# Attention from q and k laid out by the host with the head dimension first, scores as 64-row fp32 products

## The chip, the cores and the metric

One core of one Trainium2 chip runs the program. The metric is the device time of one execution in microseconds (us). The kernel before took 1429.79 us, the median of three runs (1424.49 to 1429.9). The profiled execution used below took 1432.03 us; its span from the first to the last instruction is 1429.9 us.

## The reference

Retention-like attention over 8 sequences of 576 tokens with 8 heads of 64, then two expert layers (8 experts each, 512 to 1024 to 512) on the 4608 tokens. The first layer routes each token to its best expert; the second deals tokens to experts by sorted logits with a fixed capacity. Only the first part is touched:

```python
scores = scale * np.matmul(q, k.transpose(0, 1, 3, 2))
gamma = 1.0 - 2.0 ** (-5.0 - np.arange(H, dtype=np.float32))
rel = pos[:, None] - pos[None, :]
Dmat = np.where(rel >= 0, gamma[:, None, None] ** rel[None, :, :], 0.0)
x = np.matmul(scores * Dmat[None], v)          # [B, H, S, D]
x = x.transpose(0, 2, 1, 3).reshape(B * S, H * D)
x = moe2(moe(x))
```

## The kernel before

The 4608 tokens are 36 tiles of 128; nine tiles make two sequences, so tile 4 of each nine holds the end of one sequence and the start of the next. Inside a tile the scores are computed in full; what came earlier in the sequence enters through a 64 x 64 state per head that the tiles accumulate in PSUM (`st`) and that ScalarE copies into the block-diagonal `bd`.

The order on every engine is the order in which the program is written. A tile passes through these steps, and the loop over T (L526) mixes the steps of different tiles:

- `load_tile` (L225) queues on SyncE three loads of k, q, v (rows = tokens, pieces of 64 words). It runs three tiles ahead; each of the three has four buffers.
- `s_tr` (L292): GpSimd makes `kd` (k times a decay, L298). TensorE transposes k and q by head pairs (L304, eight transposes into two PSUM tiles `tp`). ScalarE and VectorE split the transposed k and q into a high and a low fp32r part (L307, L308, L312, L315); q's two heads are put on zeroed halves, `QP`, which borrows the weight tiles w2_0 and w2_1.
- `s_qk` (L327): for each of the four head pairs three fp32r products (high-high, high-low, low-high) of 128 rows by 256 columns into `s0`, `s1` (L338), twelve in all. VectorE multiplies by the decay table `dt` into `sm` (L342).
- `s_qs` (L319): VectorE makes `qs`, the decayed transposed q (L325).
- `s_pv` (L345): state times query (L353, four fp32 products) and v times `sm` (L357, eight fp32 products, the two heads of a pair on two column halves). ScalarE copies the result to `xT` (L360).
- `s_state` (L363): eight fp32 products add the tile to the state (L375), ScalarE copies it to `bd` (L381).
- `s_out` (L384): four router products of 32 columns (L395) into the PSUM bank `lg`, four transposes of `xT` (L401), ScalarE copies and the sum of squares. `s_sel` (L407): one small product (L410) sums the router's parts into logits.
- `route`, pulled step by step by `pump` (L486), turns a group of five tiles into slots; GpSimd scatters the rows to `xs` (L471). After the fifth group SyncE loads the early rows of expert 0 (`load_x`, L480).

At T = 31 the first four weight loads of the experts are queued (`w_load`, L552), and at T = 31 to 34 ScalarE and GpSimd convert one each (`w_conv`, L180 and L181). After the loop come the last routing steps, an overflow test that reads a value into all engines, and the expert layers from about 257 us on.

The eight PSUM banks of the stage hold: `lg` one, `tp` three, `s0`, `s1`, `o`, `st` one each.

## Time and profile before

| | us | 
|---|---|
| median of three runs | 1429.79 |
| profiled execution, device time | 1432.03 |
| its span | 1429.9 |
| attention, main stretch | 40 to 220 |
| attention and routing, last part | 206 to 257 |
| expert layers | 257 to 1430 |

Engines are PE (TensorE products), PEld (its weight loads), DVE (VectorE), ACT (ScalarE), POOL (GpSimd) and SP (SyncE, which issues loads). A busy share says how long an engine had an instruction in work. Durations of products include the way through the array and overlap; the distance between the starts of one group and the next tells what a group costs. An fp32 product leaves two records, a transpose and an fp32r product one. PEclk is the clock granted to TensorE; 1.00 is 2.4 GHz and 0.50 is 1.2 GHz.

### The profile page before, as it was taken

What the parts mean: (1) busy time and instruction counts of PE and PEld (TensorE: products, weight loads), DVE (VectorE), ACT (ScalarE), POOL (GpSimd) and SP (SyncE); (2) the same over time, 40 slices, a digit from 0 to 9 for tenths busy, and PEclk for the clock granted to TensorE, in tenths of its full rate; (3) what the DMA queues carried; (4) which work ended last, traced back from release to release, by engine and by line L of the source; (5) the groups of instructions that cost most, each with busy time, mean ns of one, the idle gap of its engine ahead of it and who ended that gap; (6) DMA issues with size and microseconds to landing.
All of it is one profiled execution on the core that took longest, in us unless ns stands there. A gap on an engine that the chain in (4) does not pass through costs nothing.

```text
span 1429.9 us, 24542 instructions
## 1 busy us (share of the span) xinstructions
PE 1313.7 (92%) x9505; PEld 1140.1 (80%) x9505; DVE 847.7 (59%) x2226; ACT 521.9 (37%) x993; POOL 513.4 (36%) x460
## 2 busy tenths in 40 slices
PE   7999997799999999999999588897989898989998
PEld 6888886779898989999898476685868676777996
DVE  6787885565463646455344666675767767674320
ACT  5777775323333333333331122221213222222421
POOL 2133325442433434343320133333252534336532
PEclk9999998899999999999999789897979898989999
DMA  8767773633333324333200222323040413225310
GB/s 185 172 167 184 187 198 100 239 95 123 107 111 123 114 89 130 132 94 120 96 30 16 107 68 92 93 89 96 7 168 12 148 37 106 79 74 144 105 47 33
DMA packets 166785, 154.44 MB, mean 108 GB/s; under 512 B 121992, under 2 KB 122768, under 8 KB 166529
## 3 DMA queue, kind: packets, MB, share of 16 engines
q1 hardware_dynamic: 155088, 123.23, 29.4%
q0 software_dynamic: 11568, 29.52, 6.2%
q8 instruction: 77, 1.26, 0.4%
q14 instruction: 52, 0.42, 0.1%
HBM read 120.82 MB, written 40.28 MB: 113 GB/s over the span
## 4 chain that ended last, share of the span: by engine, by line
PE 61%; DVE 15%; issue 3%; POOL 1%; ACT 1%; DMA 1%; SPq 0%; POOLq 0%; ACTq 0%
PE l L1222 16%; PE l L1303 9%; PE l L1325 8%; PE l L1166 5%; PE l L1167 5%; PE l L1168 5%; DVE ohb L987 3%; PE srb L1106 2%; DVE cmp L833 2%; PE srb L811 1%; PE tp L647 1%; PE tp L1095 1%; DVE h2l L1306 1%; PE tp L1289 1%; PE srb L993 1%
## 5 line engine op out<-in xcount | busy, mean ns | idle before, releaser
L181 POOL TENSOR_TENSOR w_0l<-raw,w_0h 128x1024 fp32r<-128x1024 f32 x31 | 74.5, 2404 | 154.7 <-ACT w_0h L180 149.3
L181 POOL TENSOR_TENSOR w_3l<-raw,w_3h 128x1024 fp32r<-128x1024 f32 x32 | 78.2, 2443 | 115.8 <-ACT w_3h L180 114.4
L181 POOL TENSOR_TENSOR w_1l<-raw,w_1h 128x1024 fp32r<-128x1024 f32 x31 | 76.3, 2462 | 120.9 <-ACT w_1h L180 120.8
L181 POOL TENSOR_TENSOR w_2l<-raw,w_2h 128x1024 fp32r<-128x1024 f32 x31 | 74.4, 2399 | 115.7 <-ACT w_2h L180 115.6
L1170 DVE SCALAR_TENSOR_TENSOR hl<-l,hh 128x320 fp32r<-128x320 f32 x128 | 62.2, 486 | 87.5 <-ACT hh L1169 86.1
L1305 ACT ACTIVATE h2h<-l 128x288 fp32r<-128x288 f32 x128 | 52.4, 413 | 164.3 <-PE l L1303 164.3
L1169 ACT ACTIVATE hh<-l 128x320 fp32r<-128x320 f32 x128 | 55.8, 436 | 150.8 <-PE l L1168 136.6
L1328 ACT ACTIVATE o<-l 128x512 f32<-128x512 f32 (+1 forms) x40 | 23.8, 596 | 215.6 <-PE l L1325 122.9
L1231 ACT ACTIVATE yr<-l,gts 128x512 f32<-128x512 f32 x40 | 27.5, 688 | 194.3 <-PE l L1222 194.3
L1306 DVE SCALAR_TENSOR_TENSOR h2l<-l,h2h 128x288 fp32r<-128x288 f32 x128 | 57.9, 453 | 55.0 <-ACT h2h L1305 54.2
L1332 POOL DMA_INDIRECT out_dram<-o,tid x40 | 42.5, 1062 | 111.6 <-ACT o L1328 80.8
L650 DVE TENSOR_TENSOR xl<-tp,xh 128x512 fp32r<-128x512 f32 (+1 forms) x41 | 27.8, 677 | 91.8 <-ACT xh L649 90.3
L298 POOL TENSOR_TENSOR kd<-kt,gk 128x512 f32<-128x512 f32 (+1 forms) x32 | 33.4, 1044 | 98.1 <-PE st L375 48.0
L342 DVE TENSOR_TENSOR sm<-s,dt 128x512 f32<-128x512 f32 (+1 forms) x80 | 49.1, 632 | 23.7 <-PE s L338 14.3
L1276 POOL DMA_INDIRECT xg<-ybuf,idx x40 | 40.9, 1023 | 57.1 <-DVE idx L1006 22.6
L987 DVE TENSOR_TENSOR ohb<-rki,i 128x640 bf16<-128x640 int32 x32 | 58.3, 1833 | 0.0
L833 DVE TENSOR_TENSOR cmp<-v,kb 128x1280 bf16<-128x1280 f32 (+1 forms) x42 | 56.5, 1346 | 0.2
L471 POOL DMA_INDIRECT xs<-xg,r_sli x36 | 35.6, 989 | 54.0 <-DVE sm L342 29.0
L1166 PE MATMUL l<-xh,w_0h 128*128 128x320 f32 x128 | 42.1, 329 | 10.3 <-DVE hl L1170 5.8
L811 PEld LDWEIGHTS <-cmp 128*128 128x128 bf16 (+1 forms) x490 | 15.5, 96 | 44.5 <-DVE cmp L833 39.0
L811 PE MATMUL srb<-oh,cmp 128*128 128x32 bf16 (+1 forms) x490 | 20.5, 179 | 33.1 <-DVE cmp L833 32.9
L1127 DVE SCALAR_TENSOR_TENSOR jk<-wz,wgb 128x512 bf16<-128x512 f32 x64 | 45.6, 712 | 0.4
(384 smaller groups left out, 4569.8 us busy)
## 6 DMA issues: line engine op xcount, KB each, us to landing
raw<-in_moe_w_dram SPq DMA_DIRECT2D x128, 512.0 KB
ybuf<-yr SPq DMA_DIRECT2D x40, 257.0 KB
xt<-xs SPq DMA_DIRECT2D x39, 261.0 KB
kt<-in_k_dram SPq DMA_DIRECT2D x32, 256.0 KB
qt<-in_q_dram SPq DMA_DIRECT2D x32, 256.0 KB
vt<-in_v_dram SPq DMA_DIRECT2D x32, 256.0 KB
wgb<-w_gate_t SPq DMA_DIRECT2D x1, 2048.0 KB
wz<-in_moe_w_dram SPq DMA_DIRECT2D x8, 256.0 KB
```

What stands on the lines that cost most here:

```text
L181: (eng or G).tensor_tensor(lo, raw, hi.bitcast(F32), op=OP.subtract)
L833: V.tensor_tensor(cmp[:, cz], bc(v, cz, nj), kb.bitcast(F32)[:, None, :].to_broadcast([128, cz.stop - cz.start, nj]), op=OP.is_ge)
L987: V.tensor_tensor(oq, rki[:, cz, None].to_broadcast([128, NSL // NQ, 64]), i64[:, None, :].to_broadcast([128, NSL // NQ, 64]), op=OP.is_equal)
L1166: P.matmul(pp, wh[:, fz], xh[:, kk, z], start=(kk == 0), stop=False)
L1167: P.matmul(pp, wh[:, fz], xl[:, kk, z], start=False, stop=False)
L1168: P.matmul(pp, wl[:, fz], xh[:, kk, z], start=False, stop=(kk == KD - 1))
L1169: A.activation(hh[:, f, z], pp, AF.Relu)
L1170: V.scalar_tensor_tensor(hl[:, f, z], pp, 0.0, hh.bitcast(F32)[:, f, z], op0=OP.max, op1=OP.subtract)
L1222: P.matmul(py, a[:, f, z], b, start=(f == 0 and n == 0), stop=(f == KF - 1 and n == 2))
L1303: P.matmul(pq, a[:, fz_], b[:, kk, z], start=(kk == 0 and n == 0), stop=(kk == KD - 1 and n == 2))
L1306: V.scalar_tensor_tensor(h2l[:, f, z], pq, 0.0, h2h.bitcast(F32)[:, f, z], op0=OP.max, op1=OP.subtract)
L1325: P.matmul(py, a[:, f, z], b, start=(f == 0 and n == 0), stop=(f == KF - 1 and n == 2))
```

## The change

- The host lays out four arrays: `kT` and `qT` per tile with the head dimension first (partition = 64 x head parity + dimension, then head pair, then token), and `kr`, `vr` per token with all heads in one row. A tile's four loads are 128 pieces of 2 KB each.
- The transposes of k and q, the splits into two fp32r parts and the zeroed halves go. `s_tr` becomes `s_kd`, which makes only `kd`.
- The scores become eight fp32 products with 64 rows: head parity 0 on rows 0 to 63 into `s0`, parity 1 on rows 64 to 127 into `s1`, in turn. The tables `dt` and `sm` are ordered by parity.
- `lg` becomes two banks, used by tile parity; `tp` has two instead of three.
- In the loop the scores of T+1 and the small router product of T-2 stand ahead of `s_pv(T)`; `s_out` for tile 0 is run at T = 1 after `prep_pe`, which moves from T = 0 to T = 1.
- The loads before the loop are reordered: kT, qT of tile 0 first, then `dt`, then v and k rows; `ident` later. The blocks of `gq` are made one by one around `kd` of tile 1. The normalised `en` is written by ScalarE instead of VectorE.

```diff
...
+        def load_tile(T, names=("kT", "qT", "kr", "vr")):
+            t = TL.setdefault(T, {})
+            for nm in names:
+                if nm in ("kT", "qT"):
+                    t[nm] = ld.tile([128, 4, 128], F32, name=nm)
+                    SY.dma_start(t[nm], c[nm][T])
+                else:
+                    t[nm] = ld.tile([128, H, D], F32, name=nm)
+                    SY.dma_start(t[nm].rearrange("p h d -> p (h d)"), c[nm][128 * T:128 * T + 128, :])
+
+        load_tile(0, ("kT", "qT"))
+        dt_t = tab.tile([128, 2, 4, 128], F32, name="dt")
+        SY.dma_start(dt_t, c["c_dt"])
+        load_tile(0, ("vr", "kr"))
...
-        load_tile(1)
+        load_tile(1, ("kT", "qT"))
+        SY.dma_start(ident, c["c_id"])
         gq_t = tab.tile([128, 4, S], F32, name="gq")
         SY.dma_start(gq_t[:, :, 64:192], c["c_gq"])
+        load_tile(1, ("vr", "kr"))
         gs_t = tab.tile([128, 4, 3], F32, name="gs")
         SY.dma_start(gs_t, c["c_gs"])
         sel = tab.tile([128, E], F32, name="sel")
         SY.dma_start(sel, c["c_sel"])
         SY.dma_start(tri_f, c["c_tri"])
-        lgt = ps.tile([128, 512], F32, name="lg")
+        lgt = [ps.tile([128, 512], F32, name=f"lg{i}") for i in range(2)]
...
-            tp = {}
-            for nm in ("k", "q"):
-                tp[nm] = ps.tile([128, 4, 128], F32, name="tp", bufs=3)
-                for hp in range(4):
-                    P.transpose(tp[nm][:, hp, :], t[nm][:, 2 * hp:2 * hp + 2, :].rearrange("p e d -> p (e d)"), ident)
-            kh = wk.tile([128, 4, 128], F32R, name="kh")
-            kl = wk.tile([128, 4, 128], F32R, name="kl")
-            A.activation(kh, tp["k"], AF.Copy)
-            V.tensor_tensor(kl, tp["k"], kh.bitcast(F32), op=OP.subtract)
-            qh, ql = QP[T % 2]
-            for e in range(2):
-                z = slice(64 * e, 64 * e + 64)
-                A.activation(qh[z, :, e, :], tp["q"][z], AF.Copy)
-            for e in range(2):
-                z = slice(64 * e, 64 * e + 64)
-                V.tensor_tensor(ql[z, :, e, :], tp["q"][z], qh.bitcast(F32)[z, :, e, :], op=OP.subtract)
-            KT[T], QT[T] = (kh, kl), (qh, ql)
-            TQ[T] = tp["q"]
...
+                V.tensor_tensor(QS[T][:, :, :nq], TL[T]["qT"][:, :, :nq], gq_t[:, :, s0:s0 + nq], op=OP.mult)
...
-            sp = [ps.tile([128, 4, 128], F32, name=f"s{a}") for a in range(2)]
+                    V.memset(sm[z, :, :, 64 - z.start:128 - z.start], 0.0)
+            sp = [ps.tile([128, 4, 128], F32, name=f"s{e}") for e in range(2)]
             for hp in range(4):
-                o = sp[hp // 2][:, 2 * (hp % 2):2 * (hp % 2) + 2, :].rearrange("p e n -> p (e n)")
-                for n, (a, b) in enumerate(((kh, qh), (kh, ql), (kl, qh))):
-                    P.matmul(o, a[:, hp, :], b[:, hp].rearrange("p e n -> p (e n)"), start=(n == 0), stop=(n == 2))
-            for a in range(2):
-                h4 = slice(4 * a, 4 * a + 4)
+                for e in range(2):
+                    r = slice(64 * e, 64 * e + 64)
+                    P.matmul(sp[e][:, hp, :], kT[r, hp, :], qT[r, hp, :], start=True, stop=True, skip_group_check=True)
+            for e in range(2):
                 for z in HALVES if i == 4 else ALL:
-                    V.tensor_tensor(sm[z, h4, z], sp[a][z, :, z], dt_t[z, h4, z], op=OP.mult)
+                    V.tensor_tensor(sm[z, e, :, z], sp[e][z, :, z], dt_t[z, e, :, z], op=OP.mult)
             SM[T] = sm
...
-                    P.matmul(op_[64 * e:64 * e + 64, hp, :], vt[:, 2 * hp + e, :], sm[:, 2 * hp + e, :],
+                    P.matmul(op_[64 * e:64 * e + 64, hp, :], vt[:, 2 * hp + e, :], sm[:, e, hp, :],
...
-            lp = lgt[:, :136]
+            lp = lgt[T % 2][:, :136]
...
-            xp = ps.tile([128, 4, 128], F32, name="tp", bufs=3)
+            xp = ps.tile([128, 4, 128], F32, name="tp", bufs=2)
...
-            rp = lgt[:, 256:256 + 80]
+            rp = lgt[pr % 2][:, 256:256 + 80]
...
-        s_tr(0)
         s_qk(0)
-        s_qs(0)
-        for m in range(3):
-            G.tensor_tensor(gq_t[:, :, 192 + 128 * m:320 + 128 * m], gq_t[:, :, 64:192],
-                            gs_t[:, :, m, None].to_broadcast([128, 4, 128]), op=OP.mult)
-        s_tr(1)
-        s_qs(1)
+        s_kd(0)
...
+        def gq_make(m):
+            G.tensor_tensor(gq_t[:, :, 192 + 128 * m:320 + 128 * m], gq_t[:, :, 64:192],
+                            gs_t[:, :, m, None].to_broadcast([128, 4, 128]), op=OP.mult)
+
+        gq_make(0)
+        s_kd(1)
+        s_qs(1)
+        gq_make(1)
+        gq_make(2)
...
-            s_pv(T)
-            pump(3 if T >= NT - 3 else 1)
-            s_state(T)
             if T + 1 < NT:
                 s_qk(T + 1)
             if T > 1:
                 s_sel(T - 2)
+            s_pv(T)
+            pump(3 if T >= NT - 3 else 1)
+            s_state(T)
             if T >= TP:
                 pump(1)
             if T + 2 < NT:
-                s_tr(T + 2)
-            if T == 0:
+                s_kd(T + 2)
+            if T == 1:
                 prep_pe()
-            elif T < NT - 1:
+            if 0 < T < NT - 1:
...
+    q, k, v = (np.asarray(inputs[n]) for n in ("q", "k", "v"))
+    laid = {nm: np.ascontiguousarray(a.transpose(0, 2, 1, 3)).reshape(N, DM) for nm, a in (("kr", k), ("vr", v))}
+    for nm, a in (("kT", k), ("qT", q)):
+        t = a.transpose(1, 3, 0, 2).reshape(4, 2, D, NT, 128)
+        laid[nm] = np.ascontiguousarray(t.transpose(3, 1, 2, 0, 4)).reshape(NT, 128, 4, 128)
...
```

## Rows read from the trace of the kernel before

**Rows 1.** The page, busy times of the span and granted clock in 40 slices.

```profile
PE 1313.7 (92%) x9505; PEld 1140.1 (80%) x9505; DVE 847.7 (59%) x2226; ACT 521.9 (37%) x993; POOL 513.4 (36%) x460
...
PEclk9999998899999999999999789897979898989999
```

**Rows 2.** Busy time by stage: stretch, its length, each engine (count), clock, DMA.

```profile
0.00:30.00 30.00, 20.16 (x153) 17.83 (x154) 18.55 (x65) 14.51 (x26) 8.60 (x15) 0.89 0.87 199
40.00:220.00 180.00, 176.07 (x2118) 156.36 (x2118) 142.96 (x315) 137.40 (x321) 56.06 (x78) 1.00 0.73 186
...
237.00:257.00 20.00, 9.57 (x62) 7.33 (x61) 8.12 (x51) 6.55 (x16) 8.86 (x14) 0.59 0.23 84
257.00:1430.00 1173.00, 1083.48 (x6897) 937.47 (x6897) 660.97 (x1761) 345.02 (x589) 427.93 (x340) 0.94 0.29 95
```

**Rows 3.** Timeline of weight loads of one tile: start, duration, engine, line, tile.

```profile
135.58 0.19 PEld L338 LDWEIGHTS s<-w_0h,kh 128*128 128x128 f32 x1
...
136.99 0.31 PEld L410 LDWEIGHTS lg<-sel,part 128*128 128x128 f32 x2
137.14 0.50 PEld L304 LDWEIGHTS tp<-ident,kt 128*128 128x128 f32 x4
137.61 0.47 PEld L304 LDWEIGHTS tp<-ident,qt 128*128 128x128 f32 x4
138.25 0.16 PEld L395 LDWEIGHTS lg<-xT,enT 128*32 128x32 f32 x8 [0.17 <-issue]
138.60 0.42 PEld L401 LDWEIGHTS tp<-ident,xT 128*128 128x128 f32 x4 [0.20 <-issue]
138.99 0.97 PEld L353 LDWEIGHTS o<-qs,bd 128*128 128x128 f32 x8
140.08 0.85 PEld L357 LDWEIGHTS o<-sm,vt 128*64 128x64 f32 x16
140.90 0.60 PEld L375 LDWEIGHTS st<-vt,kd 128*64 128x64 f32 x16
141.57 0.19 PEld L338 LDWEIGHTS s<-w_1h,kh 128*128 128x128 f32 x1
```

**Rows 4.** Timeline, first load, first TensorE work, outputs of tiles 0, 2 and 35.

```profile
1.23 0.42 SPq L234 DMA_DIRECT2D kt<-in_k_dram  x1
...
4.62 1.09 PE L304 MATMUL tp<-ident,kt 128*128 128x128 f32 x4 [4.62 <-DMA kt<-in_k_dram]
...
13.63 1.31 PE L357 MATMUL o<-sm,vt 128*64 128x128 f32 x16
...
30.43 1.06 PE L353 MATMUL o<-qs,bd 128*128 128x128 f32 x8
...
236.92 1.91 PE L353 MATMUL o<-qs,bd 128*128 128x128 f32 x8
```

**Rows 5.** Timeline of TensorE, output products of tiles 30 and 31.

```profile
200.19 1.06 PE L353 MATMUL o<-qs,bd 128*128 128x128 f32 x8
201.17 1.09 PE L357 MATMUL o<-sm,vt 128*64 128x128 f32 x16
...
206.19 1.00 PE L353 MATMUL o<-qs,bd 128*128 128x64 f32 x8
207.12 1.09 PE L357 MATMUL o<-sm,vt 128*64 128x128 f32 x16
```

**Rows 6.** Groups of instructions by line and shape, 40 to 220 us.

```profile
L353 PE MATMUL o<-qs,bd 128*128 128x128 f32 x176 | 23.2, 275 | 0.0
...
L401 PE MATMUL tp<-ident,xT 128*128 128x128 f32 x120 | 19.7, 286 | 0.0
```

**Rows 7.** Load queue 40 to 200 us, DMA 264 to 272 us, longest wait of SyncE.

```profile
q1 hardware_dynamic: 83895, 22.29, 60.4%
...
DMA packets 1553, 2.81 MB, mean 351 GB/s; under 512 B 816, under 2 KB 816, under 8 KB 1466
...
SPq L234 <- PE st L375: 78.9, 25, 4.9
```

More of the change, by code (lines that the diff above doesn't have):

```diff
@@ L47, in constants @@
     dt = np.where(rel[:, None, :] >= 0, g[None, :, None] ** np.maximum(rel, 0)[:, None, :], 0.0) / 8.0
-    same = (p[:, None] < 64) == (p[None, :] < 64)
-    dts = dt * same[:, None, :]
     s = np.arange(64, 192)
@@ L87, in moe_kernel @@
 @with_exitstack
-def moe_kernel(ctx: ExitStack, tc: tile.TileContext, q, k, v, moe_expert_emb, moe_tau, moe_w1, moe_w2,
+def moe_kernel(ctx: ExitStack, tc: tile.TileContext, moe_expert_emb, moe_tau, moe_w1, moe_w2,
                moe2_w_gate, moe2_w1, moe2_w2, c, out, dbg=None, stage=9):
@@ L223, in moe_kernel @@
         TL = {}
-        def load_tile(T):
-            pr, i = divmod(T, 9)
-            t = {}
-            for nm, src in (("k", k), ("q", q), ("v", v)):
-                x = ld.tile([128, H, D], F32, name=nm + "t")
-                n = 0
-                while n < 128:
-                    b, s = divmod(1152 * pr + 128 * i + n, S)
-                    m = min(128 - n, S - s)
-                    SY.dma_start(x[n:n + m], src[b, :, s:s + m, :].rearrange("h p d -> p h d"))
-                    n += m
-                t[nm] = x
-            TL[T] = t
-        load_tile(0)
-        bd, QP = [], []
+        def load_tile(T, names=("kT", "qT", "kr", "vr")):
[11 more added lines that the diff above has]
+        load_tile(0, ("vr", "kr"))
+        bd = []
         for i in range(2):
@@ L244, in moe_kernel @@
             bd.append(t)
-        for i in range(2):
-            t = []
-            for nm in ("h", "l"):
-                x = wts.tile([128, FF], F32R, name=f"w2_{i}{nm}").rearrange("p (a e n) -> p a e n", a=4, e=2)
-                for e in range(2):
-                    z = slice(64 * e, 64 * e + 64)
-                    if i:
-                        A.activation(x[z, :, 1 - e, :], bd[0][z], AF.Copy)
-                    else:
-                        V.tensor_copy(x[z, :, 1 - e, :], bd[0][z])
-                t.append(x)
-            QP.append(t)
         taub = tab.tile([128, 1], F32, name="taub")
@@ L297, in s_tr @@
                 kd = wk.tile([128, H, D], F32, name="kd")
-                G.tensor_tensor(kd[r0:], t["k"][r0:], gk_t[r0:, i, :, None].to_broadcast([128 - r0, H, D]), op=OP.mult)
+                G.tensor_tensor(kd[r0:], TL[T]["kr"][r0:], gk_t[r0:, i, :, None].to_broadcast([128 - r0, H, D]),
+                                op=OP.mult)
                 KDT[T] = kd
-            tp = {}
-            for nm in ("k", "q"):
-                tp[nm] = ps.tile([128, 4, 128], F32, name="tp", bufs=3)
-                for hp in range(4):
-                    P.transpose(tp[nm][:, hp, :], t[nm][:, 2 * hp:2 * hp + 2, :].rearrange("p e d -> p (e d)"), ident)
-            kh = wk.tile([128, 4, 128], F32R, name="kh")
-            kl = wk.tile([128, 4, 128], F32R, name="kl")
-            A.activation(kh, tp["k"], AF.Copy)
-            V.tensor_tensor(kl, tp["k"], kh.bitcast(F32), op=OP.subtract)
-            qh, ql = QP[T % 2]
-            for e in range(2):
-                z = slice(64 * e, 64 * e + 64)
-                A.activation(qh[z, :, e, :], tp["q"][z], AF.Copy)
-            for e in range(2):
-                z = slice(64 * e, 64 * e + 64)
-                V.tensor_tensor(ql[z, :, e, :], tp["q"][z], qh.bitcast(F32)[z, :, e, :], op=OP.subtract)
-            KT[T], QT[T] = (kh, kl), (qh, ql)
-            TQ[T] = tp["q"]
         def s_qs(T):
-            i, tq = T % 9, TQ.pop(T)
+            i = T % 9
             nq = nq_of(i)
@@ L1419 @@
         cs[name] = nc.dram_tensor(name, a.shape, mybir.dt.from_np(a.dtype), kind="ExternalInput").ap()
-    wgt = np.ascontiguousarray(np.asarray(inputs["moe2_w_gate"]).T)
-    arrays["w_gate_t"] = wgt
-    cs["w_gate_t"] = nc.dram_tensor("w_gate_t", wgt.shape, mybir.dt.from_np(wgt.dtype), kind="ExternalInput").ap()
+    q, k, v = (np.asarray(inputs[n]) for n in ("q", "k", "v"))
[3 more added lines that the diff above has]
+        laid[nm] = np.ascontiguousarray(t.transpose(3, 1, 2, 0, 4)).reshape(NT, 128, 4, 128)
+    laid["w_gate_t"] = np.ascontiguousarray(np.asarray(inputs["moe2_w_gate"]).T)
+    for name, a in laid.items():
+        arrays[name] = a
+        cs[name] = nc.dram_tensor(name, a.shape, mybir.dt.from_np(a.dtype), kind="ExternalInput").ap()
     for i, (shape, dtype) in enumerate(_OUTS):
```

26 lines of the change are left out of this document (10 added, 16 removed).

## The prediction

> **What bounds the kernel now.** I read the profile from the outside in: first the page's busy shares and the granted clock by slice, then the busy time by stage, then TensorE's order of work inside one tile, last the queues that feed it. TensorE is the busiest engine, 92% of the span [rows 1]. Split by stage [rows 2], the reader is to see three different things. From 40 to 220 us, while the attention tiles run, TensorE is busy for 176.07 of 180 us at a granted clock of 1.00 (2.4 GHz), VectorE for 142.96, ScalarE for 137.40 and GpSimd for 56.06. Before 30 us the stage is filling; from 206 to 257 us it empties, at a clock that falls to 0.59; from 257 us to the end the two expert layers run, and the change does not touch them. So the attention stage is bound by TensorE's own queue, and what the change is worth is the TensorE time that it takes out of a tile, 36 times, less what becomes late next.
>
> One tile on TensorE, read from the weight loads, which carry the true order [rows 3]: the scores take 135.58 to 136.99, that is 1.41 us for 12 products; the router's small product 0.15; the transposes of k and q 137.14 to 138.08, 0.94 us; a gap of 0.17; the router's four products and its gap 0.35; the transposes of xT 0.39; state times query 1.09; sm times v 0.82; the state update 0.67. The next tile begins at 141.57, 5.99 us after this one. Over the stage the output products start at 30.43 for tile 2 [rows 4] and at 206.19 for tile 31 [rows 5]: 175.76 us for 29 tiles, 6.06 us each. The 120 records of the xT transposes in 180 us [rows 6] are 30 tiles, 6.0 us each, the same.
>
> **Removed.** Eight transposes: 0.94 us of TensorE per tile. With them go the ScalarE copies kh and qh and the VectorE subtractions kl and ql. Those two engines were not the bound. Undiminished they would need 137.40/30 = 4.58 and 142.96/30 = 4.77 us per tile [rows 2], so they fit a period of 4.8 us even if nothing were taken from them. I cost that part at nothing.
>
> **Replaced: the scores.** Twelve full-array products go, 1.41 us. Eight fp32 products with 64 rows of contraction come; an fp32 product leaves two records (four products, x8 in [rows 3]), so 16 records, each with 128 weight columns and 128 moving columns. No row of the trace has such a product, so I bound a record's price. The nearest is state times query: 8 records on the full array from 139.0 to 140.0. It shows what limits a record: with 128 moving columns, start to start of the next group is 0.98 us (200.19 to 201.17), with 64 moving columns it is 0.93 us (206.19 to 207.12) [rows 5]. Half the moving data, 5% of the time: the record is paid by its weights, 0.93/8 = 0.116 us, say 0.117. If the two heads of a pair, on rows 0 to 63 and 64 to 127 and in two banks, overlap in weights and products, the 16 records take 8 x 0.117 = 0.94 us; if the weight loads go one after the other, 16 x 0.117 = 1.87 us. What speaks for overlap is the neighbour on the other axis: the state update puts its two heads on two column halves, and its 16 records need 0.60 us, 0.038 each, where half of 0.117 would be 0.058 [rows 3]. Weight loads on two halves do overlap there. I take 0.94 and keep 1.87 for the range.
>
> The Trainium skill has a sentence for each side. "TensorEngine Tiling (Array Packing)", Key Properties, says that different tiles can execute weight loads and matmuls in parallel; the state rows agree for column halves, and by that the scores cost 0.94 us. "TensorE: Matmul & The Clock Gate", LDWEIGHTS, says that a load is timed by its columns and not by its contraction rows; the 64-column pair above agrees that weights set the price, and if halves of rows share nothing, that rule gives the 1.87 us. The tiling page also says that a change of tiling mode drains the engine; the gaps of 0.17 us around the router are of that kind.
>
> **Order and gaps.** Full-array, half-array and quarter-array shapes alternate. A change of shape shows as 0.07 us (state update to scores) up to 0.20 us (router to transposes) [rows 3]. Before there are four such changes in a tile; after there are five, since the scores now have a shape of their own: plus 0.07 to 0.20, I take 0.15. Net per tile: 0.94 + (1.41 - 0.94) - 0.15 = 1.26 us. Period 6.06 - 1.26 = 4.80 us.
>
> **Moved, and the wait it adds.** The scores of tile T+1 and the small router product now stand ahead of sm times v of tile T. What waits behind them is the whole rest of tile T, and they themselves wait for kT and qT of T+1 and for VectorE to have read the two score banks. That reading ends about 1.5 us after the scores before, and there are some 3.9 us of other TensorE work in between; the state copies on ScalarE (about 1.6 us after sm times v) are covered by state update, router, transposes and scores, about 2.5 us. In steady state I cost the move at nothing; without the cover it is 0.5 to 1 us per tile. SyncE issues one load more per tile and is covered by its waits for buffers [rows 7]; GpSimd keeps its work per tile. Two router banks take away the short waits on the shared one, under 0.1 us per tile.
>
> **Loads.** Per tile SyncE issues four loads of 256 KB instead of three: 1.05 MB, plus 0.27 MB scattered (128 rows of 522 words), 1.32 MB. The old loads are pieces of 256 B. Their queue moved 22.29 MB in 160 us at a share of 60.4% [rows 7], 231 GB/s while busy; the weight stream with 4 KB pieces ran at 351 GB/s [rows 7]. The new pieces are 2 KB. Between those ends 1.32 MB cost 3.8 to 5.7 us per tile. I take the end near 351, since a row of 2 KB is nearer to 4 KB than to 256 B, and since loads now wait for free buffers (78.9 us of waiting on the state update [rows 7]), not for transfers. Covered, then, at 4.8 us; the other end is a rival.
>
> **Start.** Now sm times v begins at 13.63 for tile 0 and the output of tile 2 at 30.43 [rows 4], with TensorE at half clock for part of it (0.89 over 30 us [rows 2]). After: the first load was used 3.4 us after its issue (issue 1.2, use 4.62 [rows 4]), so the first scores run at about 4.5. The bytes up to kT and qT of tile 1 are 2.15 MB, 6.1 us at 351 GB/s plus some 2.5 of first delay: 8.6 us. Then at half clock scores 1.9, output 1.7, state 1.2: 13.4. Tile 2's kT and qT (3.6 MB in) are there at 12.8. One more tile with the router's preparation, 5 to 7 us: output of tile 2 at about 20. Gain 10 us, 5 to 13.
>
> **End.** Tile 31 to tile 35 is 206.19 to 236.92 [rows 4, 5]: 30.73 us, 6.5 more than four periods. Weight loads for the first expert (2 MB), the early rows of expert 0 (0.67 MB) and the last tiles' loads meet here. The router's small product now stands ahead of the routing step, so a group's routing starts one tile earlier, and on SyncE the early rows, with their wait for GpSimd's scatters, come ahead of the weights and of tile 35's loads. That is 1.9 us more at 351 GB/s before ScalarE's first weight conversion, and xT stands behind that conversion; with the shorter tile the wait may be 1 to 4 us. An earlier routing gains about as much at the end. I keep the 6.5 and count only the four tiles: 5.0 us. After the last tile the routing chain and the expert layers are the same: nothing.
>
> **Sum.** 29 x 1.26 = 36.5, start 10, end 5.0: 51.5 us. The profiled execution took 1432.03 us (span 1429.9 and 2.1 around it): 1380.5. The median of the runs, 1429.79, lies 2.2 lower: 1378. I say 1379. Its own range, from gaps, start and end, is 1366 to 1392.
>
> **Rivals.**
> 1. Weight loads of the two row halves do not overlap. Scores 1.87 us, net gain per tile 0.94 + 1.41 - 1.87 - 0.15 = 0.33. 29 x 0.33 = 9.6, start 6, end 1: 17 us, about 1414. For it: 0.93 against 0.98 us. Against it: 0.038 us per record in the state update.
> 2. Transfers become the bound at 231 GB/s: 5.7 us per tile, gain 33 x 0.36 = 12 plus 4 at the start, about 1415. Against it: 351 GB/s for long pieces.
> 3. Slower: every step from one row half to the other waits until the earlier record has left the array. A record then costs its whole duration, 0.275 us [rows 6]; 16 x 0.275 = 4.4 us, period 8.26, 33 x 2.2 = 73 us lost, about 1502. It decides from 0.166 us per record on, where 16 records (2.65 us) eat the transposes and the start. Against it: column halves alternate in the same way at 0.038 and 0.051 us [rows 3].
> 4. The change does what it says, but the gain ends in the emptying stage, because the transfers at 206 to 257 us set its end: near 1428. Against it: these transfers are issued tile by tile and move with the tiles.
>
> **How the numbers follow.** Forecast 0.62, rival 1 0.22, rival 2 0.09, rival 3 0.04, rival 4 0.03. The range 1366 to 1416 takes in nearly all of the forecast and the middle of rivals 1 and 2. A measurement here tells 0.5%, about 7 us, from no change. Faster: 0.62 + 0.22 + 0.09 = 0.93; same 0.03; slower 0.04.
>
> **What would show it.** In the trace after: no records of transposed k and q; 16 score records within 0.9 to 1.1 us (right) or 1.8 to 2.0 (rival 1); a tile every 4.8 us; TensorE still near 100% busy at 1.00, with load waits on buffers and not on transfers; the output of tile 2 near 20 us; the span after the last tile unchanged. The forecast is wrong if TensorE shows gaps in mid-stage ended by a load or by the score evacuation, or if the score records stand 0.117 us apart or more.

## The result, and the profile after

The changed kernel takes 1390.15 us (median of 4 runs, 1386.43 to 1391.43) against 1429.85 for the kernel before beside it: a ratio of 0.9726, 95% interval 0.9697 to 0.9756, a gain of 39.7 us. The forecast was 1379 and its own range 1366 to 1392, so the time lies inside it, near its upper end. The profiled execution took 1389.89 us, its span is 1387.8, so between the two profiled executions 42.1 us are gone.

The page of the changed kernel first: busy time, share and count of each engine, and the granted clock in 40 slices. It answers to [rows 1].

```profile
PE 1268.4 (91%) x9361; PEld 1094.1 (79%) x9361; DVE 776.2 (56%) x2113; ACT 460.5 (33%) x882; POOL 515.9 (37%) x460
...
PEclk9999978999999999999999598997979898989999
```

TensorE lost 45.3 us of busy time and is still the busiest by far; VectorE lost 71.5 and ScalarE 61.4. The busy time by stage (stretch, its length, each engine with its count, clock, DMA share, GB/s) answers to [rows 2]:

```profile
0.00:30.00 30.00, 20.45 (x208) 18.06 (x208) 14.17 (x56) 10.12 (x21) 10.32 (x16) 1.00 0.82 270
40.00:150.00 110.00, 109.50 (x1572) 93.09 (x1569) 68.46 (x183) 68.55 (x182) 43.88 (x61) 1.00 0.87 285
192.00:257.00 65.00, 44.80 (x274) 41.15 (x274) 37.70 (x139) 20.14 (x44) 32.56 (x60) 0.79 0.50 167
```

In mid-stage TensorE is busy for 109.50 of 110 us at the full clock: the tiles are bound by its own queue, as before. VectorE, 79% busy before, is at 62%. One tile in the timeline of weight loads answers to [rows 3]:

```profile
92.38 0.97 PEld L304 LDWEIGHTS s<-qT,kT 64*128 64x128 f32 x16 [0.17 <-issue]
93.47 0.30 PEld L375 LDWEIGHTS lg<-sel,part 128*128 128x128 f32 x2
93.69 0.97 PEld L318 LDWEIGHTS o<-qs,bd 128*128 128x128 f32 x8
94.78 0.85 PEld L322 LDWEIGHTS o<-sm,vr 128*64 128x64 f32 x16
95.60 0.60 PEld L340 LDWEIGHTS st<-vr,kd 128*64 128x64 f32 x16
96.27 0.16 PEld L360 LDWEIGHTS lg<-xT,enT 128*32 128x32 f32 x8
96.63 0.42 PEld L366 LDWEIGHTS tp<-ident,xT 128*128 128x128 f32 x4 [0.20 <-issue]
97.21 0.41 PEld L304 LDWEIGHTS s<-qT,kT 64*128 64x128 f32 x6 [0.17 <-issue]
```

The transposes of k and q are gone, the 16 score records take 0.97 us (1.09 to the next group), and the next tile begins 4.83 us later. The output products, in the timeline of TensorE, answer to [rows 4, 5]; these are tile 2, tile 31 and tile 35, and the first product of expert 0's second layer:

```profile
26.42 1.14 PE L318 MATMUL o<-qs,bd 128*128 128x128 f32 x8
...
164.35 1.08 PE L318 MATMUL o<-qs,bd 128*128 128x64 f32 x8
...
191.82 1.14 PE L318 MATMUL o<-qs,bd 128*128 128x128 f32 x8
...
255.26 0.47 PE L1191 MATMUL l<-w_0h,hh 128*128 128x512 f32 x1
```

So the gain is earned and given back in four places. Tile 2 starts at 26.42 where it was 30.43: 4.0 us. From tile 2 to tile 31 pass 137.93 us instead of 175.76: 37.8 us, a period of 4.756. From tile 31 to tile 35 it is 27.47 instead of 30.73: 3.3 us. The second layer of expert 0 began at 297.2 and now begins at 255.3, 42.0 earlier, though tile 35 and the first expert product (256.90, now 211.88) were 45.0 earlier: 3 us are lost again. 4.0 + 37.8 + 3.3 - 3.0 = 42.1. The two products in the timeline of TensorE in the kernel before:

```profile
256.90 0.63 PE L1166 MATMUL l<-xh,w_0h 128*128 128x320 f32 x1 [4.56 <-ACTq L666]
...
297.24 0.47 PE L1222 MATMUL l<-w_0h,hh 128*128 128x512 f32 x1
```

### The profile page after: what moved, and what is told of

Read it like the earlier page. It is cut to its first block, busy times and chain, and to the rows that moved or that the text cites. A ratio compares the mean times of both kernels' runs of the same rounds, so it can differ in the third digit from the quotient of the medians.

```text
span 1387.8 us, 23937 instructions
## 1 busy us (share of the span) xinstructions
PE 1268.4 (91%) x9361; PEld 1094.1 (79%) x9361; DVE 776.2 (56%) x2113; ACT 460.5 (33%) x882; POOL 515.9 (37%) x460
## 4 chain that ended last, share of the span: by engine, by line
PE 54%; DVE 15%; issue 12%; POOL 3%; ACT 1%; DMA 1%; POOLq 0%; another core or an unknown queue 0%; ACTq 0%
PE l L1191 12%; PE l L1272 9%; PE l L1294 8%; PE l L1135 5%; PE l L1136 5%; PE l L1137 5%; DVE ohb L956 3%; DVE cmp L802 2%; PE srb L1075 2%; PE srb L780 1%; DVE h2h L1277 1%; PE tp L616 1%; PE l L1288 1%; DVE h2l L1275 1%; PE srb L962 1%
## 5 line engine op out<-in xcount | busy, mean ns | idle before, releaser
L1301 POOL DMA_INDIRECT out_dram<-o,tid x40 | 42.3, 1057 | 113.3 <-ACT o L1297 81.9
L281 POOL TENSOR_TENSOR kd<-kr,gk 128x512 f32<-128x512 f32 (+1 forms) x32 | 34.5, 1081 | 60.1 <-PE st L340 25.0
L304 PE MATMUL s<-qT,kT 64*128 64x128 f32 x576 | 45.2, 298 | 9.3 <-DMA qT<-qT 8.1
L956 DVE TENSOR_TENSOR ohb<-rki,i 128x640 bf16<-128x640 int32 x32 | 50.2, 1577 | 0.0
```

Source lines behind the costliest of these rows:

```text
L956: V.tensor_tensor(oq, rki[:, cz, None].to_broadcast([128, NSL // NQ, 64]), i64[:, None, :].to_broadcast([128, NSL // NQ, 64]), op=OP.is_equal)
```

## The experiments

The kernel before took 1423.7 and 1424.5 us beside the first two batches of runs, and 1432.1 and 1422.1 beside the last two, so each run is read against the kernel before of its own batch; the first two batches (e0 to e8) ran on one chip, the last two on others. Where it helps, I name the start of the output products of tiles 2, 31 and 35 from the trace of TensorE.

**The yardstick.** The changed kernel once more, nothing edited.

> The changed kernel as it is, once more, on the chip of the runs beside it, as their yardstick. If a ratio to the kernel before carries over from chip to chip, it is 0.9726 of that chip's kernel before, and the two small edits run earlier (qs later: 0.9715, weights earlier: 0.970) were worth 1 to 4 us. Rival: it comes out at 0.970 to 0.971 here, and those two edits were worth nothing that can be told.

1387.63 us, ratio 0.9745 (0.9724 to 0.9767). Tiles 2, 31 and 35 start at 26.41, 163.76 and 190.53. Its kernel before stood within 1 us of that of e1 to e4, so these can be compared with 1387.6 by their medians, to some 3 us. By stage the traces scatter as well: where the start is not edited, tile 2 starts at 25.25 to 26.65 (the changed kernel twice, e4, e12), and where the end is not edited, tile 31 to tile 35 takes 26.77 to 28.05 us (the changed kernel twice, e3). Smaller differences in these two tell nothing.

**e1: scores with all of one row half first.** The eight products of rows 0 to 63 run one after the other, then those of rows 64 to 127.

```diff
-            for hp in range(4):
-                for e in range(2):
+            for e in range(2):
+                for hp in range(4):
```

> The changed kernel with the eight score products in another order: all four head pairs of parity 0 (rows 0 to 63) first, then all four of parity 1 (rows 64 to 127). The same products, the same bytes. Theory (the two row halves overlap because neighbours in the queue lie on different halves): neighbours on one half cannot overlap, 16 records take 16 x 0.117 = 1.87 us instead of about 1.0, a tile takes 4.8 + 0.9 = 5.7 us, the kernel 36 x 0.9 = 32 us more, about 1422. Rival (the low price of a record comes from the 64 rows alone, whatever stands beside it): no change, 1390, records 0.06 us apart.

1398.78 us, ratio 0.9822 (0.9782 to 0.9862), 11 us above the yardstick. Weight loads of one tile:

```profile
91.94 1.52 PEld L304 LDWEIGHTS s<-qT,kT 64*128 64x128 f32 x16 [0.16 <-issue]
93.58 0.30 PEld L375 LDWEIGHTS lg<-sel,part 128*128 128x128 f32 x2
```

The same 16 records take 1.52 us where alternating halves took 0.97. Halves of rows do overlap, as the forecast held; but a record alone costs 0.095 us, not the 0.117 of a full-array record, so the overlap saves 0.55 us a tile and not 0.9. The cost fell between the two expectations. The 11 us understate it: from tile 2 to tile 31 pass 153.3 us instead of 137.4, 15.9 or 29 x 0.55, and the start and the end are 1.6 and 4.3 us shorter here. The Trainium skill, "TensorEngine Tiling (Array Packing)", Key Properties, lets different tiles load and multiply in parallel; the trace agrees for row halves. "TensorE: Matmul & The Clock Gate", LDWEIGHTS, times a load by its columns alone; 0.095 us for 64 rows against 0.117 for 128 rows of the same 128 columns speaks against that here.

**e2: the transposes alone.** The kernel before, with q and k laid out by the host and no transposes; split copies, 12 fp32r score products, order of a round and the single router bank stay. For want of room kT and qT have two buffers each; no wait of TensorE from 40 to 180 us ends on a load.

```diff
-            tp = {}
-            for nm in ("k", "q"):
-                tp[nm] = ps.tile([128, 4, 128], F32, name="tp", bufs=3)
-                for hp in range(4):
-                    P.transpose(tp[nm][:, hp, :], t[nm][:, 2 * hp:2 * hp + 2, :].rearrange("p e d -> p (e d)"), ident)
+            tp = {"k": t["kT"], "q": t["qT"]}
```

> The kernel before with one part of the change: the host's layout (kT, qT, kr, vr) and no transposes of q and k; scores stay twelve fp32r products, the order of the loop, one router bank and the order of the loads stay those of before. The loads of kT and qT have two buffers each for want of room. Theory (TensorE time adds up): a tile goes from 6.06 to about 5.1 us, the attention stage gains 33 x 0.94 = 31 us, the start some 3, about 1396 us; the scores then are worth the rest, 0.4 us per tile. Rival (another engine binds as soon as the transposes go: VectorE needs 4.77 and ScalarE 4.58 us per tile here): a tile stays above 5.4 us, about 1407 or more.

1414.73 us, ratio 0.9936 (0.9914 to 0.9958): 9 us by the medians, where 29 tiles by 0.94 us would give 27; in the traces tiles 2 to 31 gain 14.6 us. The busy time of 80 us in mid-stage; from the waits of 40 to 180 us, those of TensorE and of its weight loads for the router (in total, times, longest); and the output products of two tiles:

```profile
100.00:180.00 80.00, 74.36 (x938) 65.73 (x930) 73.22 (x153) 66.11 (x158) 32.34 (x43) 1.00 0.75 245
```

```profile
PEld lg L388 <- ACT lgs L404: 11.3, 25, 0.5
PE lg L388 <- ACT lgs L404: 9.1, 25, 0.4
```

```profile
100.69 1.06 PE L346 MATMUL o<-qs,bd 128*128 128x128 f32 x8
...
106.18 1.06 PE L346 MATMUL o<-qs,bd 128*128 128x128 f32 x8
```

The mean period is 5.56 us (tile 2 at 27.36, tile 31 at 188.57), TensorE has gaps, and VectorE is now busy for 73.22 of 80 us, 92%. That share suggests VectorE as the new bound, but the waits don't show it. An ordinary tile takes 5.49 us. The old one took 5.99; less 0.94 that is 5.05, and the 0.45 us that the weight loads stand in each tile (11.3 in 25) for ScalarE's copy out of the single router bank make it 5.50. Waits of TensorE that end on VectorE come to 1.7 us in all 25 tiles. So what keeps this kernel from cashing the 0.94 us is the wait at the single bank, in this order of work; that the split copies do it is not shown here.

**e9: the copies put back.** Whether the copies cost anything, from the other side: the changed kernel with VectorE's and ScalarE's share of the split as dead work.

```diff
         def s_qs(T):
...
+            A.activation(act, kT, AF.Copy)
+            V.tensor_tensor(dve, kT, kT, op=OP.subtract)
+            for z in HALVES:
+                A.activation(act[z], qT[z], AF.Copy)
+                V.tensor_tensor(dve[z], qT[z], qT[z], op=OP.subtract)
```

> The changed kernel with the work of the split put back on its engines alone: in each tile ScalarE copies k and q (one copy of 128 rows, two of 64) and VectorE subtracts as often, into buffers that nobody reads; TensorE's work and the loads are as in the changed kernel. Theory, after the run with the transposes alone taken out: VectorE's 3.0 us a tile become about 5.2, more than the 4.75 us period, so the period is 5.2 to 5.6 us and the time 15 to 28 us above the changed kernel. Rival, the prediction's own step (what ScalarE and VectorE stop doing is worth nothing): the copies find room beside TensorE, period 4.75 to 4.85, time within 4 us.

1409.86 us, ratio 0.9841 (0.9819 to 0.9863), against 0.9726 and 0.9745 of the changed kernel: 14 to 16 us. Busy time in mid-stage, and the output products of two tiles in the timeline of TensorE:

```profile
30.00:150.00 120.00, 113.35 (x1485) 95.96 (x1485) 109.32 (x233) 103.58 (x235) 42.11 (x53) 0.93 0.72 240
```

```profile
91.80 2.01 PE L326 MATMUL o<-qs,bd 128*128 128x128 f32 x8
...
97.56 1.14 PE L326 MATMUL o<-qs,bd 128*128 128x128 f32 x8
```

VectorE is at 91%, ScalarE at 86%, and the mean period is 5.43 us (26.71 to 184.25). Many tiles still take 4.83; the rest is lost in stalls, 12 of the 19.6 us in two stretches in which VectorE has steps of the routing to do as well (75.7 to 97.6 and 132.5 to 147.9). After a stall TensorE's clock is at half for a while: the same eight records take 2.01 us at 91.80 and 1.14 at 97.56, and the granted clock of the stretch is 0.93. The dead subtractions read SBUF, where the old ones read PSUM and took 690 ns. Most of them take as long, but some that stand beside GpSimd take far longer (two in 2.87 us at 132.79), and the means are 769 and 787 ns; so the old copies would cost less, by how much no run shows. Nor does the run separate the two engines: from 30 to 180 us TensorE's waits end mostly on ScalarE's logits copy (2.9 us) and on VectorE's mask product (2.6). The rival, the forecast's own step, is refuted.

**e5: the old order of a round.** Value products, router step and state of tile T again ahead of the scores of tile T+1; all else as changed.

```diff
+            s_pv(T)
+            pump(3 if T >= NT - 3 else 1)
+            s_state(T)
             if T + 1 < NT:
                 s_qk(T + 1)
             if T > 1:
                 s_sel(T - 2)
-            s_pv(T)
-            pump(3 if T >= NT - 3 else 1)
-            s_state(T)
```

> The changed kernel with the order of a round undone: value products, router step and state of tile T again ahead of the scores of tile T + 1. Theory of the prediction (the new order is worth about nothing): the mask product of VectorE still has the selection, router and transposes of tile T - 1 (2.9 us of TensorE) to hide behind; period stays 4.8 us, time within 3 us of the changed kernel. Rival: with the tile at 4.8 us instead of 6.06 that cover is too short, TensorE waits for VectorE's masked scores 0.3 to 1 us in each tile, and the time rises by 10 to 36 us.

1382.94 us, ratio 0.9709 (0.9683 to 0.9735), 4.7 us under the yardstick; the span, 1379.4, is 5.1 under. In the steady state the order is worth nothing, as forecast: 4.728 us a tile against 4.736 for the yardstick. The new order costs at the ends. Tile 2 starts at 24.47 instead of 26.41, tile 31 to 35 takes 25.96 instead of 26.77, and the first expert product to the second layer 42.1 instead of 44.3. Neither expectation had a gain. Of the 5.1 us, 2.7 lie at the two ends, each just outside the scatter given above; the last 2.2 lie in an expert stretch that comes and goes with edits elsewhere (e12), so they are not shown to be the order's.

**e6: one router bank.** As changed, with one PSUM bank for the router's products.

```diff
-        lgt = [ps.tile([128, 512], F32, name=f"lg{i}") for i in range(2)]
+        lgt = [ps.tile([128, 512], F32, name="lg0")] * 2
...
-            xp = ps.tile([128, 4, 128], F32, name="tp", bufs=2)
+            xp = ps.tile([128, 4, 128], F32, name="tp", bufs=3)
```

> The changed kernel with one PSUM bank for the router's products instead of two (the bank goes to a third buffer of the transposes). Theory of the prediction: two banks are worth under 0.1 us a tile, so 0 to 4 us more than the changed kernel. Rival, from the run with the transposes alone taken out, where TensorE stood 9.1 us in 25 tiles before the router products for ScalarE's copy out of the single bank: 0.36 us a tile, 12 us more, and TensorE's router products (line 360) again wait for ScalarE's copy.

1388.55 us, ratio 0.9742 (0.9716 to 0.9768): no difference from the yardstick, the period is 4.765. The second bank is worth nothing measurable. The 0.36 us of e2 belong to its order of work: there the small router product stands directly ahead of the four router products, with no transposes between them.

**e3 and e4: one edit at each end.** e3 puts the scaled queries of tile 1 behind the first masked scores on VectorE. e4 loads the first expert's weights from tile 29 on instead of 31.

```diff
-        s_qs(1)
...
+            if T == 0:
+                s_qs(1)
```

> The changed kernel with VectorE's qs of tile 1 moved behind the evacuation of tile 1's scores (from before the loop to behind the scores in the loop's first pass). Theory (at the start TensorE's scores of tile 2 wait from 15.0 to 16.2 us and again to 16.7 because qs(1), which waits for a table of GpSimd until 14.0, stands on VectorE ahead of sm(1), whose scores were there at 12.2): scores of tile 2 run at about 15.0 without a pause, the output products of tile 2 start 2 to 3 us earlier than 26.4, time 1387 to 1388. Rival (TensorE's half clock and the loads set the start, the queue does not): below 0.5 us.

```diff
-WL, LX, GE = (31,5,4)
+WL, LX, GE = (29,5,4)
```

> The changed kernel with the first four weight loads queued two tiles earlier (at T = 29 instead of 31), ahead of the early rows of expert 0 on SyncE; the conversions stay where they are. Theory (ScalarE waits 6.8 us at 169.8 to 176.6 for the first weights, whose load stands on SyncE behind the early rows, which wait for a scatter; TensorE then stands for 4.4 us): that wait goes, tiles 31 to 35 take 23 to 24 us instead of 27.5, time about 1386. Rival (loads of the last tiles are late instead, or the routing chain after the last tile sets the end): below 1 us.

e3: 1383.95 us, 3.7 under the yardstick; ratio 0.9715 (0.9686 to 0.9743). Tile 2 starts at 23.39 instead of 26.41, and those 3.0 us are kept: tile 31 starts at 160.74. e4: 1382.55 us, 5.1 under; ratio 0.970 (0.9669 to 0.973). Tile 31 to tile 35 takes 24.86 us instead of 26.77; another 1.2 us of its lead are in the start, which e4 does not touch. The start and the end of the stage each hold back a few us that one line moves. What stands there, the trace of the changed kernel shows. At the start, the timelines of GpSimd, VectorE and TensorE:

```profile
12.93 1.04 POOL L479 TENSOR_TENSOR gq<-gq,gs 128x512 f32<-128x512 f32 x1 [3.07 <-DMA gs<-c_gs]
13.94 1.04 POOL L281 TENSOR_TENSOR kd<-kr,gk 128x512 f32<-128x512 f32 x1
14.94 2.50 POOL L479 TENSOR_TENSOR gq<-gq,gs 128x512 f32<-128x512 f32 x2
...
14.01 1.51 DVE L291 TENSOR_TENSOR qs<-qT,gq 128x512 f32<-128x512 f32 x1 [1.53 <-POOL gq L479]
15.45 1.27 DVE L307 TENSOR_TENSOR sm<-s,dt 128x512 f32<-128x512 f32 x2
...
10.13 2.08 PE L304 MATMUL s<-qT,kT 64*128 64x128 f32 x16 [3.78 <-DMA qT<-qT]
...
16.18 2.67 PE L304 MATMUL s<-qT,kT 64*128 64x128 f32 x16 [1.21 <-DVE sm L307]
18.78 2.07 PE L318 MATMUL o<-qs,bd 128*128 128x128 f32 x8
```

The scores of tile 2 wait for VectorE to have read the banks of tile 1, VectorE stands behind qs of tile 1, qs behind a table of GpSimd, and that behind a 6 KB load. But e3, which takes qs out of that queue, does not gain in the way that was expected. Its timeline of TensorE:

```profile
16.75 1.16 PE L304 MATMUL s<-qT,kT 64*128 64x128 f32 x16 [1.54 <-DMA qT<-qT]
...
23.39 1.14 PE L318 MATMUL o<-qs,bd 128*128 128x128 f32 x8
```

The scores of tile 2 were to run at 15.0; they run at 16.75, later than the 16.18 of the changed kernel, since they now wait for the load of their queries. The gain comes behind them: from these scores to the output of tile 2 pass 6.64 us instead of 10.24, because the scores run in one piece and at full clock (1.5 us less) and so do the products behind them (2.1 us less). So VectorE's queue and the loads end this wait within 1 us of each other, and the half clock behind it costs more than the wait itself. Why the clock is full here after 1.54 us of wait and at half in the changed kernel after 1.21 is not shown. At the end, the timelines of ScalarE and TensorE:

```profile
176.58 1.06 ACT L177 ACTIVATE w_0h<-raw 128x1024 fp32r<-128x1024 f32 x1 [6.82 <-DMA raw<-in_moe_w_dram]
...
179.29 0.59 PE L375 MATMUL lg<-sel,part 128*128 128x8 f32 x2 [4.42 <-ACT part L363]
179.73 2.05 PE L318 MATMUL o<-qs,bd 128*128 128x128 f32 x8
```

ScalarE waits 6.82 us for raw weights with the router's copies queued behind; TensorE stands 4.42 us and comes back at half clock. In e4 that conversion starts at 169.47 without such a wait. Part of the gain is paid back: the state update of tile 31 there waits 1.82 us for GpSimd, and the clock is at half at 170.56.

**e11: the start without loads.** Tiles 1 and 2 use tile 0's buffers.

```diff
-        load_tile(1, ("kT", "qT"))
+        TL[1] = dict(TL[0])
...
-        load_tile(1, ("vr", "kr"))
...
-        load_tile(2)
+        TL[2] = dict(TL[0])
```

> The changed kernel with tiles 1 and 2 read from tile 0's buffers: it leaves out the loads of tiles 1 and 2 (2 MB), so these two tiles have tile 0's queries, keys and values. Theory: the first 26 us are set by the loads, which fill 0.9 of the DMA time; without 2 MB of them (5 to 7 us at the 280 to 400 GB/s there) the output of tile 2 starts at 19 to 22 us instead of 26.4, and all of that is gained, 4 to 7 us. Rival: VectorE's and GpSimd's order and the half clock hold the start; then the output of tile 2 starts at 24 us or later and the gain is under 2.5 us.

Only the first 27 us are read, since other data sends the tokens elsewhere and the later stages grow (1941.52 us). Tile 2 starts at 26.86 us: with 2 MB fewer loads nothing is gained, and the theory that the loads alone set the start falls. Its timelines of GpSimd, VectorE and TensorE:

```profile
11.57 1.04 POOL L280 TENSOR_TENSOR kd<-kr,gk 128x512 f32<-128x512 f32 x1
12.57 2.05 POOL L478 TENSOR_TENSOR gq<-gq,gs 128x512 f32<-128x512 f32 x2
...
11.70 0.92 DVE L100 TENSOR_TENSOR nw_r<-nw_r,nw_u 8x1 f32<-8x1 f32 x1
12.66 0.97 DVE L101 TENSOR_TENSOR nw_r<-nw_r,nw_t 8x1 f32<-8x1 f32 x1
...
16.23 0.62 DVE L290 TENSOR_TENSOR qs<-qT,gq 128x512 f32<-128x512 f32 x1
...
17.50 2.67 PE L303 MATMUL s<-qT,kT 64*128 64x128 f32 x16 [4.23 <-DVE sm L306]
```

With the loads early, GpSimd's products run back to back from 9.57 to 15.6, and a VectorE operation on eight numbers, 0.15 us elsewhere, takes 0.92 and 0.97 us: it ends with GpSimd's operation. The chain on the expert embeddings, which stands ahead of qs and sm of tile 1, so ends at 16.2. TensorE waits 4.23 us for it.

**e8: both ends and a warm start.** e3 and e4 together, and 19 products on a constant, 7 ahead of and 12 behind the first scores, to have the clock up.

```diff
+        warm = tab.tile([128, 512], BF, name="warm")
+        V.memset(warm, 1.0)
...
+        dummy(7)
         s_qk(0)
+        dummy(12)
```

> The changed kernel with three edits at its ends: the scaled queries of tile 1 behind the first masked scores, the first expert's weights two tiles earlier, and 19 products of 512 columns on a constant ahead of and behind the first scores, to have TensorE's clock up when tile 1 comes. If the start lost its 6 us to VectorE's order and the low clock, and the end 1.7 us to weights that came late, the output of tile 2 starts at 21 to 23 us instead of 26.4, and the whole is 6 to 9 us under the changed kernel. Rival: tile 2 is set by its loads (the queries of tile 1 landed at 10.1 us), or what is won is waited off in the first expert; then 0 to 4 us.

1379.81 us, ratio 0.9683 (0.9661 to 0.9705): 7.8 us under the yardstick, their intervals do not touch, and the fastest kernel of this study. e3 and e4 alone sum to 8.8, so the warm products show no gain: the scores of tiles 0 and 1 do run at full clock (1.16 us), but tile 2 starts at 24.09, later than in e3, since its scores wait 3.29 us until 15.90 for the load of their queries and the clock is at half again at 17.5.

**e12: products ahead of the first expert.** Products on a constant in TensorE's waits before the expert: 6 ahead of each of the last two rank steps, 2 behind each of the last two transposes.

```diff
+            if pr >= len(GRP) - 2:
+                warm(6)
             rp = lgt[pr % 2][:, 256:256 + 80]
...
             xsplit(ps.tile([128, KD, 128], F32, name="tp"), 0, t, 0, r)
+            if t:
+                for _ in range(2):
+                    P.matmul(wm, onesb, onesb[:, None, :].to_broadcast([128, 4, 128]), start=True, stop=True,
+                             skip_group_check=True)
```

> The changed kernel with products of 512 columns on a constant in the waits of TensorE ahead of the first expert (6 ahead of each of the last two rank steps, 2 behind each of the last two transposes), which change no other work. Theory: 3 us are lost in the first expert because TensorE's clock stays at half for 8.0 us behind the first product (5.4 and 2.9 us in other kernels); with TensorE busy ahead of it the clock is up at the first product or within 3 us, and the stretch from the first expert product to the first product of its second layer is 41 to 42 us instead of 44.3; time 2 to 3 us down. Rival: the 4.5 us idle that stays directly ahead of the first product keeps the clock at half all the same; stretch 43 to 45 us, time within 1.5 us.

From the first expert product (213.0) to the second layer (254.9) it is 41.9 us, as the theory said, 2.4 less than in the yardstick. But e5 and e8 reach 42.1 and 41.5 without such products. What goes with the length in all kernels of this study but e11, whose expert starts from other data, is an idle stretch behind the first three or four expert products, which the profile ends with nothing; in the timeline of the changed kernel:

```profile
211.88 0.64 PE L1135 MATMUL l<-xh,w_0h 128*128 128x320 f32 x1 [4.48 <-ACTq L635]
...
212.85 0.47 PE L1135 MATMUL l<-xh,w_1h 128*128 128x320 f32 x1
214.63 0.64 PE L1136 MATMUL l<-xl,w_1h 128*128 128x320 f32 x1 [1.32 <-issue]
```

The seven kernels with that stretch (1.3 to 1.9 us: the changed kernel, its yardstick, e1, e3, e4, e6, e9) need 43.1 to 44.3 us, the six without it or with 0.2 us of it (before, e2, e5, e8, e12, e13) 40.3 to 42.3. So e12 doesn't separate the clock from the stretch. On the whole time it is inconclusive too: 1387.22 us is the yardstick's own time, but the ratio, 0.9669 (0.9645 to 0.9694), is lower than the changed kernel's, since the kernel before took 1432.1 in that batch; the changed kernel was not run in it.

**e13: what the runs pointed to.** The old order of e5, weights from tile 29, the chain on the embeddings behind tile 1, and the tables of the queries loaded ahead of tile 1.

```diff
-WL, LX, GE = (31,5,4)
+WL, LX, GE = (29,5,4)
...
+        SY.dma_start(gs_t, c["c_gs"])
+        SY.dma_start(gq_t[:, :, 64:192], c["c_gq"])
         load_tile(1, ("kT", "qT"))
...
+            if T == 0:
+                prep_en()
```

> What the runs point to, together: the old order of a round (4.7 us under the changed kernel by itself), the first expert's weights two tiles earlier (about 3 us by itself), and a start in which VectorE's chain on the expert embeddings (12 steps that stand ahead of the scaled queries and masked scores of tile 1) comes behind tile 1, and the tables of the scaled queries load ahead of tile 1. Theory: VectorE's and GpSimd's order, not the loads, holds the start, so the output of tile 2 starts at 20 to 22.5 us (26.4 in the changed kernel, 24.5 with the old order alone), and the whole is 8 to 11 us under the changed kernel, a ratio of 0.965 to 0.968. Rival: the loads or the half clock hold it at 24 us or later, and the ratio is 0.969 or more.

1384.53 us, ratio 0.9723 (0.9686 to 0.976): the theory's place was right and its sum wrong. The timeline of TensorE:

```profile
12.49 1.16 PE L318 MATMUL o<-qs,bd 128*128 128x128 f32 x8
...
19.43 0.59 PE L495 MATMUL lg<-ident,en 8*128 8x8 f32 x4 [2.87 <-ACT en L478]
...
21.80 1.91 PE L318 MATMUL o<-qs,bd 128*128 128x128 f32 x8
...
28.49 1.06 PE L318 MATMUL o<-qs,bd 128*128 128x128 f32 x8
...
169.58 1.12 PE L340 MATMUL st<-vr,kd 64*64 64x64 f32 x16 [3.39 <-POOL kd L281]
170.63 2.08 PE L304 MATMUL s<-qT,kT 64*128 64x128 f32 x16
```

Tile 1 starts at 12.49 (18.78 in the changed kernel) and tile 2 at 21.80, as expected (a chain and two loads moved at once, so the run does not tell which of them did it); but the moved chain now stops TensorE for 2.87 us, the clock is at half afterwards, and tile 3 starts at 28.49, where e5 had 29.21. At 169.58 the state update waits 3.39 us for GpSimd, whose product had waited 7.28 us for the load of kr, now in one stretch with the weights, and the clock falls again. The first expert product is at 211.4, later than e5's 207.0.

## Why the prediction was right, and where it was not

The sum was 51.5 us, the profiled executions differ by 42.1. The start is short by 6.0, the end by 1.7, 3.0 are lost after the last tile, and the steady state gave 1.3 more.

**The bound and the period.** Right. TensorE is 99.5% busy at the full clock in mid-stage, and the period is 4.756 us for a forecast of 4.80; 37.8 us for 36.5. Some of that is luck. An ordinary tile went from 5.99 to 4.83 us, 1.16 instead of 1.26: the scores took 0.03 us more than forecast, the changes of shape 0.06 more. 29 tiles by 1.16 are 33.6 us; the other 4 are stalls between ordinary tiles that became fewer, which the forecast did not cost.

**The scores.** Right in size: 0.97 us for 0.94. Right in mechanism: e1 takes the overlap away and pays for it. The other bound was mis-sized: 16 records one after the other take 1.52 us, not 1.87, so rival 1's world lies 0.55 us a tile from the changed kernel, 15.9 us in mid-stage and 11 in all (e1), not the 35 that the forecast put between them.

**The copies, costed at nothing.** Wrong as a step, without harm to the sum. I divided busy time by tiles, 4.58 and 4.77 us, saw that it fits into 4.80 and let it stand. e9 shows what that mean hides: an ordinary tile does stay at 4.83 us, but the tiles with routing steps stall and the mean becomes 5.43. The removal of the copies carries up to 0.7 us (5.43 less 4.756) of the 1.3 us that a tile lost; how much less, with copies that read PSUM, is open.

**Order and banks.** Right in mid-stage, both nothing (e5, e6). Wrong at the ends for the order: the kernel without it is 4.7 us faster, some 2.7 of them at the two ends, which no part of the forecast held.

**The loads.** Right. From 40 to 150 us the queues move 285 GB/s at a share of 0.87, so 1.32 MB cost about 4.0 us of a tile of 4.76, and no wait of TensorE ends on a load there.

**The start.** Wrong: 4.0 us for a forecast of 10, under its range of 5 to 13. The steps that failed are the load time of tile 1 and, above all, "One more tile with the router's preparation, 5 to 7 us". The scores of tile 1 ran at 10.13, when their queries had landed, and not at 8.6, so tile 0 was through at 15.0 instead of 13.4. The output of tile 2 then came 11.4 us later: a wait of 1.2 us that ends on VectorE, and 10.24 us of scores with a pause and products at half clock, which e3 does in 6.64. The forecast chained loads and TensorE alone, and put the clock back to full too early. Left out were the queues of VectorE and GpSimd (e11), where two operations had moved: the products that make the query tables, and qs, which now reads both operands from SBUF. Which of queue and load ends the wait changes from run to run (e3, e8).

**The end.** 3.3 us for 5.0. The forecast named the wait, early rows ahead of the weights on SyncE and ScalarE's conversion behind, put it at 1 to 4 us, and then let an earlier routing pay for it. ScalarE waited 6.82 us, and queuing the weights two tiles earlier (e4) gets 1.9 us of the stretch back.

**After the last tile.** "Nothing" was wrong by 3.0 us. The loss lies between the first expert product and the second layer and goes with 1.3 us of idle time that no event in the profile ends and a longer time at half clock. What decides whether it appears is open: it comes and goes with edits that do not touch the experts.

## What to carry to other kernels

When work is taken off the bound, add up the next engines' busy time per round, and for the rounds with extra work apart from the mean: with VectorE at 91% and ScalarE at 86% ordinary tiles kept their 4.83 us, and the mean still rose to 5.43. A busy share does not tell what holds the queue; at 92% in e2 the waits ended elsewhere. Stages that fill and empty have their own chains; follow each engine's queue there, the small preparations included, and don't scale the steady state. And a few us won at one end were lost again as soon as a stall elsewhere halved TensorE's clock, so edits that each pay alone have to be run together.

## What the runs showed of the hardware

Two things came unexpected. First, VectorE and GpSimd stop each other, and whether they do depends on where VectorE's operands lie. The product qs, with q in PSUM, took at most 693 ns in the kernel before; with q in SBUF its 32 instances take between 418 and 2223 ns. The line's own view in the kernel before and in the changed one (count, minimum, median and maximum in ns, first and last start, forms):

```profile
L325 DVE TENSOR_TENSOR qs<-tp,gq x32: 424/692/693, 16.4 to 228.1; 128x512 f32<-128x512 f32 x28, 128x256 f32<-128x256 f32 x4
```

```profile
L291 DVE TENSOR_TENSOR qs<-qT,gq x32: 418/686/2223, 14.0 to 181.8; 128x512 f32<-128x512 f32 x28, 128x256 f32<-128x256 f32 x4
```

The mask product sm, one operand in PSUM, keeps its 0.69 us beside the same GpSimd work, and eight numbers in SBUF take 0.97 us while GpSimd works. The Trainium skill, "SBUF — State Buffer", Who interferes with whom, says so: a VectorE instruction with two SBUF inputs contends with a GpSimd instruction that reads SBUF, one with at most one such input doesn't outside the two-port modes, and the shared ports are an exclusive lock. The traces agree. Had I asked where the change moves qs's operand, the start would have been costed nearer.

Second, fp32 weight loads of 64 rows on alternating row halves come 0.061 us apart (0.97/16), on the same half 0.095 (1.52/16), on column halves 0.038 [rows 3], on the full array 0.117. Half the rows cost less with the same columns, and two halves in turn less than one half twice.
